# Running a block pipeline, and the next batch's attention, earlier in a one-core attention and mixture-of-experts kernel

## The chip, the cores and the metric

The kernel runs on one core of a Trainium2 chip. The time is the device time of one execution in microseconds (us). The median of the kernel before is 515.28 us; its profiled execution has a span of 514.3 us, and the time is one to two microseconds above the span. Ratios between kernels are the mean time of one kernel's fast runs over the mean of the other's fast runs in the same rounds, so they are not quite the ratio of the medians quoted beside them. The experiments ran in three groups, each on one chip and with runs of the kernel before beside them: tie, gate_early, pool_first and before_tail; left_last, pool_best, pool_best2 and pool_best2_gate; after_again, pool_best3 and no_late_w.

The engines are PE (matmul), PEld (its weight loads), DVE (vector), ACT (scalar), POOL and SP (here only a queue that issues DMA).

## The reference, cut to what matters

```python
# linear attention over 8 batches, 8 heads, 576 tokens, 64 columns
phi = lambda x: where(x > 0, x, exp(x) - 1) + 1
kv  = einsum('bhsd,bhse->bhde', phi(k), v);  z = sum(phi(k), axis=2)
x   = einsum('bhsd,bhde->bhse', phi(q), kv) / (phi(q) @ z + 1e-6)   # -> 4608 tokens x 512
# four experts, every token goes through all of them
for e in range(4):
    out += p[:, e:e+1] * (relu(x @ w1[e]) @ w2[e])      # w1 512x1024, w2 1024x512
```

## The kernel before

The 4608 tokens are nine tiles of 512. Tile j is 512 tokens of batch j; tile 8 holds the 64 "leftover" tokens of each batch. A unit (j, e) is one expert on one tile. It has a first layer, a hidden activation `h`, and a second layer that adds into `acc`.

There are two ways to compute a unit. The plain one takes 32 matmuls of 512 columns in each layer. The other takes seven block products instead of eight (a Strassen-like scheme): 56 matmuls of 256 columns in each layer, plus sums of blocks. The class `Block` is half a first layer in that scheme; `layer2_product` is a piece of the second.

```python
class Block:                       # cut
    def p1(self): ... self.products(self.b, ...); self.e5 = self.bank("e"); nc.scalar.copy(self.e5, self.b)
    def p2(self): ... nc.scalar.activation(self.h[:, :, 0, 0:NH], self.e5, AF.Relu)
    def p6(self): ... self.u2 = self.copy("u2", 2)          # ACT copies PSUM to SBUF
    def p7(self): ... self.u3 = self.copy("u3", 1)
    def p5(self): ...
    def c22(self): add_relu(self.h[:, :, 1, NH:NT], self.e5, self.u3)   # DVE
    def p4(self): ... nc.scalar.activation(..., AF.Relu)
    def p3(self): ... add_relu(self.h[:, :, 0, NH:NT], self.e5, self.u2)
```

The kernel before uses the plain scheme for all of tile 0 and for unit (1, 0), and the block scheme for the other 31 units. Batch 1's attention runs near the end of tile 0, and batch 2's is pressed into the last three units of tile 1. From tile 2 on there is a steady state. Work is put at positions counted in slots (one block product each), sorted, and emitted between block products.

```python
def run(end):
    while work and work[-1][0] < end:          # strictly below the next slot
        g = work.pop()[2]; g[0](*g[1:])
slot = 0
for n in range(len(blocks) + 1):
    ...
    for own, name in ((True,"p1"),(False,"p7"),(False,"p5"),(True,"p2"),(False,"p4"),(True,"p6"),(False,"p3")):
        getattr(x, name)(); ...
        slot += 1
        run(slot)
```

The weights are loaded, and cast from 32-bit to 16-bit, by DMA issued from POOL. Batch 1's inputs are issued from POOL too, behind all weights. Inputs of the later batches, and all outputs, go through the SP queue:

```python
for r in range(6): load_w(0, r)                 # weights, POOL queue
for e in range(1, E):
    for r in range(4): load_w(e, r)
b1.load_left("k", "v", "q", eng=nc.gpsimd)      # batch 1, POOL queue, behind them
for (n, i), home in zip(ORDER, homes): b1.load(n, i, nc.gpsimd, home=home)
```

In the second layer of the block scheme, a running sum and a side sum share one bank of PSUM (the memory, divided into banks, that the matmuls write to): `run, side = pys[i][:, 0:DH], pys[i][:, DH:Dm]`.

## Time and profile before

| stretch (us) | what runs | length | PE work, counted | PE gap |
|---|---|---|---|---|
| 24.08 to 64.23 | tile 0, plain | 40.15 | 40.17 | 0.0 |
| 64.23 to 93.73 | batch 1's attention, last of tile 0, first layer of (1, 0) | 29.50 | 24.33 | 5.2 |
| 93.73 to 136.83 | block pipeline fills, batch 2's attention | 43.10 | 34.30 | 8.8 |
| 136.83 to 149.37 | first unit of tile 2 | 12.54 | 12.23 | 0.3 |
| 149.37 to 486.88 | to the last block | 337.51 | 335.55 | 2.0 |

"PE work, counted" is a sum over the matmul records of the stretch: 0.216 us for each of 512 columns, 0.109 for 256, and about 0.056 for the small ones of the attention. These are the distances from start to start in full stretches of the PE's timeline. The gap is the length less that sum. I count this way because the page's busy time of the PE overstates: records overlap, and a matmul at half clock counts as busier.

The first fence is from the page of the kernel before: the span in 40 slices of 12.86 us, in tenths (PE busy, granted PE clock, DMA share), and the GB/s that the DMA engines moved.

```profile
PE   6799978889999999999999999999999999999994
PEclk9799999998999999999999999999999999999998
DMA  8999933737254425452445244623231020001003
GB/s 251 208 208 207 228 123 124 213 114 119 48 164 144 106 58 146 144 110 57 145 144 110 55 144 145 108 45 118 83 67 27 2 83 1 1 22 63 1 1 83
```

The second is the busy time by stretches of the same kernel. The columns are the stretch, its length, the busy time (and number of instructions) of PE, PEld, DVE, ACT and POOL, then granted clock, DMA share and GB/s. The DMA share adds up the times of all packets, so it can pass 1.

```profile
24.08:64.23 40.15, 40.15 (x190) 18.35 (x189) 18.16 (x32) 18.32 (x31) 14.36 (x21) 1.00 1.11 213
64.23:93.73 29.50, 25.36 (x165) 13.18 (x164) 19.58 (x50) 18.75 (x39) 7.43 (x12) 1.00 0.46 148
93.73:136.83 43.10, 38.07 (x305) 28.70 (x304) 31.31 (x63) 31.21 (x63) 20.41 (x17) 0.96 0.52 116
136.83:188.50 51.67, 51.46 (x488) 45.76 (x486) 41.69 (x92) 38.10 (x78) 41.79 (x39) 1.00 0.43 116
```

From 137 us on the PE is full. The room for a gain lies between 64 and 137 us. And until about 64 us the DMA engines are full at some 207 GB/s.

The third fence is the end of the PE's timeline. Columns: start, length, engine, line, operation, output<-inputs, size, count.

```profile
500.62 1.33 PE L611 MATMUL py<-t,hs 128*128 128x256 f16 x8
501.80 1.33 PE L611 MATMUL py<-w,h 128*128 128x256 f16 x8
502.96 1.33 PE L611 MATMUL py<-t,hs 128*128 128x256 f16 x8
```

A pair of products takes 1.17 us from start to start, where eight matmuls need 0.87.

### The profile page before, as it was taken

How to read it: one execution, taken by the hardware profiler on the slowest of the kernel's cores; microseconds unless marked ns; L12 is line 12 of the kernel's file. 1: busy time of each engine (PE TensorE's matmuls, PEld its weight loads, DVE VectorE, ACT ScalarE, POOL GpSimd, SP SyncE). 2: the span in 40 equal slices, each digit the busy share in tenths (PEclk: the TensorE clock that was granted, in tenths of full speed). 3: DMA queues.
4: the chain of work that ended last, by engine and by line, in shares of the span. 5: the costliest groups of instructions: out<-in, count | busy, mean ns of one | idle time of the engine just before them, and what ended most of it. 6: DMA issues, size and time to landing. Idle time of an engine off the chain costs nothing.

```text
span 514.3 us, 11256 instructions
## 1 busy us (share of the span) xinstructions
PE 489.0 (95%) x4199; PEld 397.7 (77%) x4199; DVE 366.0 (71%) x787; ACT 324.2 (63%) x647; POOL 345.8 (67%) x340
## 2 busy tenths in 40 slices
PE   6799978889999999999999999999999999999994
PEld 3444444467788888898889888888988888888873
DVE  5544586359986879687968796889688756775684
ACT  5653475995589559955895599559954465446520
POOL 2522522146796698669866986698668977987781
PEclk9799999998999999999999999999999999999998
DMA  8999933737254425452445244623231020001003
GB/s 251 208 208 207 228 123 124 213 114 119 48 164 144 106 58 146 144 110 57 145 144 110 55 144 145 108 45 118 83 67 27 2 83 1 1 22 63 1 1 83
DMA packets 80935, 54.29 MB, mean 106 GB/s; under 512 B 46224, under 2 KB 73872, under 8 KB 80880
## 3 DMA queue, kind: packets, MB, share of 16 engines
q1 hardware_dynamic: 71760, 41.64, 30.8%
q0 software_dynamic: 9120, 11.93, 12.0%
q8 instruction: 33, 0.54, 0.4%
q14 instruction: 22, 0.18, 0.1%
HBM read 45.16 MB, written 9.44 MB: 106 GB/s over the span
## 4 chain that ended last, share of the span: by engine, by line
PE 80%; DVE 8%; ACT 5%; DMA 2%; issue 2%; SPq 2%; DVEq 0%; ACTq 0%
PE py L611 34%; PE pb L673 19%; PE pe L673 14%; PE ph L472 5%; PE py L527 5%; DVE acc L518 3%; DVE x_sb L397 2%; PE psum_kv L374 1%; DMA rawu<-in_v_dram 1%; SPq L239 1%; DMA qT<-qp 1%; PE psum_nd L414 1%; DVE h L657 1%; ACT u L684 1%; ACT vp L295 1%
## 5 line engine op out<-in xcount | busy, mean ns | idle before, releaser
L518 DVE SCALAR_TENSOR_TENSOR acc<-py,p_sb,acc 128x256 f32<-128x256 f32 (+1 forms) x390 | 184.0, 487 | 62.0 <-PE py L611 48.9
L583 POOL TENSOR_TENSOR hs<-h 128x512 f16<-128x512 f16 x62 | 72.0, 1161 | 67.7 <-DVE h L657 67.7
L657 DVE CUSTOM_DVE_ANT_0 h<-pe,u 128x512 f16<-128x512 f32 x124 | 85.4, 689 | 36.2 <-PE pe L673 19.1
L673 PEld LDWEIGHTS <-w 128*128 128x128 f16 x992 | 96.3, 98 | 16.3 <-issue 2.9
L611 PEld LDWEIGHTS <-h 128*128 128x128 f16 x992 | 97.3, 98 | 14.9 <-issue 2.7
L611 PE MATMUL py<-w,h 128*128 128x256 f16 x744 | 107.4, 274 | 0.7 <-DVE acc L518 0.2
L585 POOL TENSOR_TENSOR hs<-hs,h 128x512 f16<-128x512 f16 x62 | 71.7, 1156 | 24.8 <-PE py L611 22.2
L684 ACT COPY u<-pb 128x512 f32<-128x512 f32 x124 | 73.1, 590 | 22.4 <-PE pb L673 20.0
L611 PEld LDWEIGHTS <-hs 128*128 128x128 f16 x744 | 71.8, 98 | 11.3 <-issue 2.9
L673 PEld LDWEIGHTS <-s 128*128 128x128 f16 x744 | 72.5, 98 | 9.3
L611 PE MATMUL py<-t,hs 128*128 128x256 f16 x496 | 74.4, 272 | 1.2 <-DVE acc L518 1.0
L673 PE MATMUL pb<-tt,w 128*128 128x256 f16 x496 | 74.6, 273 | 0.9 <-ACT u L684 0.9
L589 POOL TENSOR_TENSOR hs<-h,hs 128x512 f16<-128x512 f16 x62 | 71.7, 1157 | 3.2 <-PE py L611 3.2
L587 POOL TENSOR_TENSOR h<-h 128x512 f16<-128x512 f16 x62 | 72.2, 1164 | 0.0
L699 ACT ACTIVATE h<-pe 128x512 f16<-128x512 f32 x62 | 37.0, 598 | 53.2 <-PE pe L673 52.6
L693 ACT COPY pe<-pb 128x512 f32<-128x512 f32 x62 | 35.9, 579 | 46.7 <-PE pb L673 43.1
L527 PE MATMUL py<-w,h 128*128 128x512 f16 x160 | 38.4, 379 | 0.8 <-DVE acc L518 0.8
L472 PE MATMUL ph<-xT,w 128*128 128x512 f16 x160 | 38.3, 387 | 0.9 <-ACT xT L451 0.9
L717 ACT ACTIVATE h<-pb 128x512 f16<-128x512 f32 x62 | 36.9, 595 | 1.3 <-PE pb L673 1.2
L673 PE MATMUL pe<-tt,s 128*128 128x256 f16 x248 | 37.5, 274 | 0.0
L673 PE MATMUL pb<-tt,s 128*128 128x256 f16 x248 | 37.2, 273 | 0.0
L516 ACT ACTIVATE acc<-py,p_sb 128x256 f32<-128x256 f32 (+1 forms) x64 | 31.4, 508 | 7.5 <-PE py L527 4.2
(102 smaller groups left out, 635.0 us busy)
## 6 DMA issues: line engine op xcount, KB each, us to landing
out_dram<-acc SPq DMA_DIRECT2D x32, 256.0 KB, 2.4
w<-in_moe_w_dram POOLq DMA_DIRECT2D x14, 512.0 KB, 19.6
rawb<-in_v_dram SPq DMA_DIRECT2D x26, 256.0 KB, 2.9
rawb<-in_q_dram SPq DMA_DIRECT2D x26, 256.0 KB, 2.9
rawb<-in_k_dram SPq DMA_DIRECT2D x26, 256.0 KB, 2.8
w<-in_moe_w_dram POOLq DMA_DIRECT2D x4, 256.0 KB, 7.2
rawb<-in_v_dram POOLq DMA_DIRECT2D x4, 256.0 KB, 3.6
out_dram<-acc SPq DMA_DIRECT2D x8, 128.0 KB, 2.3
```

What stands on the lines that cost most here:

```text
L472: nc.tensor.matmul(out=ph, lhsT=w1_sb[e][:, dc, fj * P : (fj + 1) * P], rhs=xT_of(j)[:, dc], start=(dc == 0), stop=(dc == DC - 1),)
L518: nc.vector.scalar_tensor_tensor(out=acc, in0=ps, scalar=pscal, in1=acc, op0=AO.mult, op1=AO.add)
L527: nc.tensor.matmul(out=py, lhsT=rows(hT, fj)[:, ns * P : (ns + 1) * P], rhs=w2_sb[e][:, fj, :], start=(fj == 0), stop=(fj == FC - 1),)
L583: nc.gpsimd.tensor_tensor(out=hs[0], in0=a21, in1=a22, op=AO.add)
L585: nc.gpsimd.tensor_tensor(out=hs[1], in0=hs[0], in1=a11, op=AO.subtract)
L587: nc.gpsimd.tensor_tensor(out=a21, in0=a11, in1=a21, op=AO.subtract)
L589: nc.gpsimd.tensor_tensor(out=hs[3], in0=a12, in1=hs[1], op=AO.subtract)
L611: nc.tensor.matmul(out=ps, lhsT=lhsT(k), rhs=rhs[:, k], start=first and k == 0, stop=k == FH - 1, skip_group_check=True,)
L657: nc.vector._custom_dve(TENSOR_ADD_SAT, out=out, in0=ps, in1=u, s0=BIG, s1=0.0)
L673: nc.tensor.matmul(out=ps[:, kk], lhsT=lk(kc), rhs=rhs[:, kc], start=first and kk == 0 and kc == 0, stop=kc == 1, skip_group_check=True,)
L684: nc.scalar.copy(u, self.b)
L699: nc.scalar.activation(self.h[:, :, 0, 0:NH], self.e5, AF.Relu)
```

## The change

The intent is to start the block pipeline at tile 0's second expert. Tile 0's plain second layers then feed the PE while the pipeline fills. Batch 1's attention is spread over the slots of tile 0, batch 2's gets the steady schedule, and the last unit gets separate PSUM banks. Batch 1's loads move to the SP queue, behind a small DMA that reads a finished `h` (a gate). The diff, cut to its core (the tuned numbers of the positions are mostly left out):

```diff
+    "DMA": ('w100', 'w101', 'w102', 'w103', 'w220', 'w200', 'w201', 'w110', 'w111', 'w121', 'w120',
+            'w210', 'w211', 'w130', 'w131', 'w221', 'w230', 'w231'),      # layer, expert, piece
+    "WGATE": ('q', 3),
+    "BLK": (-1.0, 7.0, 14.0, 21.0, 28.0, 35.0, 53.0),
 ...                                       # ATTN[0], batch 1: k from 21.9, lk 19.9, v from 26.0, q from 33.4
+            g=(14.1, 14.3),
+    def load_first():                      # weights start when q's last piece of batch 0 is there
+        nc.gpsimd.tensor_copy(out=scr[:, 0:1], in_=b0.raw[tuple(CFG["WGATE"])][:, 0, 0, 0:1])
+        for x in CFG["DMA"]: load_w(*map(int, x[1:]))
+    def gate(i):
+        nc.sync.dma_start(out=scr[0:1, ...], in_=latest["h"][0:1, 0, 0, 0:8].bitcast(FP32))
-        b1.load_left("k", "v", "q", eng=nc.gpsimd)
-            b1.load(n, i, nc.gpsimd, home=home)
+            put(at["g"][0], bt.load_left, "k", "v", "q")              # SP queue, behind the gate
+                put(at["g"][n == "q"], bt.load, n, i, nc.sync, homes[m])
-            if self.b >= 2:                # phi of batch 1: Identity and Exp on ACT, one DVE pass
+            if self.b >= 1:
 ...                                       # qT and xT of batch 1: PE transposes, evacuated by ACT
+        if (j, e) == (NTILES - 1, E - 1):  # last unit: running and side sums in separate banks
+            if p == 2:
+                pys[i] = [ppm.tile([P, DH], FP32, tag=tag, bufs=2, name=f"p{tag}") for tag in ("b", "e")]
+            run, side = pys[i]
+        def put_block(at, *g):             # block products are now entries of the same sorted list
+            for pos, name in ((0,"p1"),(3,"p2"),(5,"p6"),(8,"p7"),(9,"p5"),(9.1,"c22"),(11,"p4"),(13,"p3")):
+                put_at(at + pos, getattr(bl, name))
 ...
         work.sort(key=lambda w: w[0:2])
+        for _, _, g in work: g[0](*g[1:])
```

## The prediction

> **What bounds the kernel now.** From 137 us on, the PE: busy time by stretches shows PE at 51.46 of 51.67 us for one tile at full clock (DVE 41.7, ACT 38.1, POOL 41.8). The Trainium skill ("Perfetto Trace Analysis", Identifying the Most-Contended Engine) calls matmul busy time a bad measure, so I count issue times from the PE's timeline: 0.216 us per N=512 matmul, 0.109 per N=256, about 0.055 per small attention matmul.
> - 24.08 to 64.23 us (tile 0, plain): full.
> - 64.23 to 93.73 (batch 1's attention, last tile-0 expert, tile 1's first layer 1): 24.4 us of work in 29.5, 5 us of bubbles. The waits name late batch-1 data (PE waits 2.6 us for the POOL cast of vl) and ACT/DVE chains.
> - 93.73 to 136.83 (block pipeline fills; plain layer 2, weight sums and batch 2's attention squeezed in): 34.2 us of work in 43.1, 9 us of bubbles.
> - Tail, 499.4 to 507.7: product pairs take 1.17 us where the PE needs 0.87. Running and side sums share one PSUM bank, so PE and DVE alternate, as the skill ("PSUM — Partial Sum Buffer", PSUM bank collisions) says two engines on one bank must.
>
> **What the change does.**
> 1. Layer 1 of tile 0's experts 1 to 3 and both layers of tile 1's expert 0 go from 32 N=512 matmuls (6.91 us) to 56 N=256 (6.1): about -3.8 us of PE work net of extra transposes, all on the critical path.
> 2. The pipeline fills while tile 0's plain layer 2 feeds the PE, batch 1's attention spreads over 36 slots, batch 2 gets the steady schedule. Most of the 14 us of bubbles should go.
> 3. Costs: batch 1's phi takes an extra 0.64 us ACT pass (8 times), qT/xT evacuations go to ACT (0.59 each), tile 0's token sums to DVE; six blocks take 2.95 us ACT and 1.38 us DVE each; nearly all 32 weight sums (0.68 to 0.92 us) must fit before tile 1. In the batch-1 stretch I estimate ACT 31 and DVE 33 us against 31 us of PE work, with all attention going through two PSUM banks. Remaining bubbles: 6 us (estimate).
> 4. DMA: weights start when q's last piece is in (about 10 us, as before); 8.4 MB at the 207 GB/s of the page's slices end near 52 us, about 5 us ahead of use. Batch 1's 3.1 MB waits on the SP queue for a gate at about 42 us and shares with the last weights.
> 5. Start: six small loads leave the SP queue (0.63 us each); v's last piece (15.3 us, on the chain) comes about 0.7 us sooner.
> 6. Tail: separate banks make pairs DVE-bound, 2 x 0.46; 7 pairs save 1.65 us.
>
> Sum, as span: 23.4 (dense layer 1 starts) + 108.0 (PE work up to the second unit of tile 2; 111.8 before) + 6 (bubbles) + 363.3 (rest, less tail) = 500.7; plus 0.9 between span and time: 501.5 us, 2.7% faster. Range 497 to 507. Chances: faster by over 2% 0.82, within 2% 0.17, slower by over 2% 0.01.
>
> **What would show it.** Tile 1 as a 51.7 us stretch with PE full; second unit of tile 2 starting near 137 us instead of 149.4; bubbles of about 6 us between 45 and 80 us, released by ACT and DVE; tail pairs at 0.93 us; first dense layer 1 at about 23.4.
>
> **What would make it wrong.** The batch-1 stretch saturating ACT/DVE or its two banks (12 us of bubbles or more gives 507); weights late for the blocks, whose sums need the whole matrix (the out-of-order w2 half costs 2.5 us); the gate opening late; granted clock falling after PE gaps (0.80 to 0.85 in some early stretches before).

## The result, and the profile after

The changed kernel takes 522.94 us (median of 4 runs, 522.69 to 525.18) against 515.28. The ratio is 1.0157, with a 95% interval of 1.0129 to 1.0186. It is slower by 1.6%; I had forecast a gain of 2.7% and a range of 497 to 507 us. The profiled span is 521.0 us, against 500.7 in my sum.

The same rows of the page, after (slices of 13.03 us):

```profile
PE   5887499989999999999999999999999999999994
PEclk9999599999999999999999999999999999999998
DMA  8999943535244425452444354624222020002003
```

The fifth slice, 52 to 65 us, has the PE at 0.4 and its clock at 0.5, and the DMA still at 0.9. By stretches, with the boundaries at the same events as before (start of dense matmuls, first block of unit (1, 0) at 92.83, second unit of tile 2 at 154.18):

```profile
22.65:50.20 27.55, 24.07 (x151) 14.14 (x151) 13.24 (x26) 15.29 (x30) 4.69 (x7) 1.00 1.18 208
50.20:66.93 16.73, 7.29 (x22) 3.10 (x22) 4.95 (x9) 6.90 (x14) 0.00 (x0) 0.59 1.08 244
66.93:92.83 25.90, 24.51 (x203) 16.55 (x202) 22.98 (x48) 19.49 (x42) 0.00 (x0) 1.00 0.37 107
92.83:115.77 22.94, 20.77 (x170) 15.29 (x167) 16.12 (x27) 22.09 (x49) 14.96 (x13) 1.00 0.51 162
```

In the second row no engine is loaded: ACT 6.90 and DVE 4.95 of 16.73 us. So the stretch is not bound by any of them. By count the PE did 3.90 us of work there and lost 12.8. ACT's waits between 45 and 70 us (total, number and longest) are

```profile
ACT kp L301 <- DMA rawb<-in_k_dram: 7.5, 1, 7.5
ACT kl L340 <- DMA rl<-in_k_dram: 4.5, 2, 3.4
```

and the PE's longest between 20 and 110 us

```profile
PE pb L722 <- ACT u L733: 6.3, 3, 5.6
PE pe L722 <- ACT pe L742: 3.9, 1, 3.9
```

ACT stands 12 us at batch 1's k, which has not come. The PE does not need that k yet. It needs ACT's copies `u` and `pe` of a block of unit (0, 2), and those stand behind k in ACT's queue. The PE's timeline shows both waits:

```profile
54.06 1.01 PE L722 MATMUL pe<-xT,w 128*128 128x256 f16 x4 [3.87 <-ACT pe L742]
54.87 2.77 PE L571 MATMUL py<-w,h 128*128 128x512 f16 x6
63.22 1.01 PE L722 MATMUL pb<-tt,w 128*128 128x256 f16 x4 [5.58 <-ACT u L733]
```

These two waits are 9.4 of the 12.8 us. The other 3.4 us are matmuls between and after them that took about twice their time, start to start (0.43 us instead of 0.216).

The DMA view between 43 and 58 us shows why k is late. q0 carries the weights and q1 batch 1's loads; the columns are packets, MB, and share of the 16 engines' time:

```profile
q0 software_dynamic: 2105, 2.60, 98.0%
q1 hardware_dynamic: 1622, 0.40, 20.5%
rawb<-in_k_dram SPq DMA_DIRECT2D x4, 256.0 KB, 11.4
```

In 15 us the SP queue got 0.40 MB through, 27 GB/s of some 200. That is about what the six leftover loads hold (six times 64 KB), which stand first in the queue; the first 256 KB piece of k, issued at 47.35 us, reached ACT at 61.5. The pieces of k took 11.4 us from issue to landing (median of four), where the whole run's median is 3.0.

There are two more losses. Between 28 and 50 us 4.8 us are lost by count (17.05 us of work in 21.82); the PE's longer waits there are for weights (2.1 us in all) and for a sum of weights on DVE (1.2 us). And one that I had not thought of: the steady tiles, which the change was not to touch, take 52.01 us instead of 51.42. The PE's timeline at the second unit of tile 2, before:

```profile
149.81 0.60 PE L611 MATMUL py<-w,h 128*128 128x256 f16 x4
150.32 0.60 PE L673 MATMUL pb<-tt,w 128*128 128x256 f16 x4
150.76 0.60 PE L611 MATMUL py<-t,hs 128*128 128x256 f16 x4
```

and after:

```profile
154.61 0.60 PE L660 MATMUL py<-w,h 128*128 128x256 f16 x4
155.43 0.60 PE L660 MATMUL py<-t,hs 128*128 128x256 f16 x4 [0.22 <-DVE acc L562]
155.86 0.60 PE L722 MATMUL pb<-tt,w 128*128 128x256 f16 x4
```

Two products have changed places, and the one now in front waits for DVE. Positions 9.0 and 10.0 of the second layer fall exactly on slots of block products. A layer-2 product of unit n at 9.0 stands at base + 14n + 20 + 9, and `p7` of the next unit's second block at base + 14(n+1) + 7 + 8, which is the same number. The old loop let the block product go first, because it ran only work strictly below the next slot. The new sorted list breaks a tie by order of insertion, and unit n's products are inserted before unit n+1's blocks.

The tail does what was expected of it:

```profile
509.08 1.04 PE L660 MATMUL pe<-t,hs 128*128 128x256 f16 x8
509.95 1.04 PE L660 MATMUL pb<-t,hs 128*128 128x256 f16 x8
510.83 1.21 PE L660 MATMUL pe<-w,hs 128*128 128x256 f16 x8
```

Pairs follow each other after 0.87 us instead of 1.17; only the last two intervals are longer, 1.04 and 1.18 us.

### The profile page after: what moved, and what is told of

Its sections match the earlier page's. It is cut to its first block, busy times and chain, and to the rows that moved or that the text cites. A ratio compares the mean times of both kernels' runs of the same rounds, so it can differ in the third digit from the quotient of the medians.

```text
span 521.0 us, 11542 instructions
## 1 busy us (share of the span) xinstructions
PE 487.7 (94%) x4327; PEld 408.4 (78%) x4327; DVE 375.6 (72%) x800; ACT 336.0 (65%) x679; POOL 345.8 (66%) x328
## 4 chain that ended last, share of the span: by engine, by line
PE 78%; DMA 9%; ACT 5%; DVE 2%; issue 2%; SPq 2%; POOL 1%; ACTq 0%; DVEq 0%
PE py L660 35%; PE pb L722 21%; PE pe L722 16%; DMA w<-in_moe_w_dram 3%; DMA rawb<-in_k_dram 3%; PE py L571 2%; DMA rawb<-in_q_dram 2%; DVE acc L562 1%; PE psum_nd L458 1%; DMA qT<-qp 1%; PE psum_kv L418 1%; SPq L244 1%; ACT vp L322 1%; ACT u L733 1%; SPq L264 1%
## 5 line engine op out<-in xcount | busy, mean ns | idle before, releaser
L722 PEld LDWEIGHTS <-w 128*128 128x128 f16 x1120 | 108.4, 98 | 30.8 <-issue 14.2
L706 DVE CUSTOM_DVE_ANT_0 h<-pe,u 128x512 f16<-128x512 f32 x140 | 96.6, 690 | 48.9 <-PE pe L722 28.4
L733 ACT COPY u<-pb 128x512 f32<-128x512 f32 x140 | 82.5, 589 | 34.4 <-PE pb L722 32.4
L722 PEld LDWEIGHTS <-s 128*128 128x128 f16 x840 | 81.9, 98 | 13.5 <-DVE s L599 1.7
L722 PE MATMUL pb<-tt,w 128*128 128x256 f16 x560 | 84.4, 273 | 7.4 <-ACT u L733 7.4
L748 ACT ACTIVATE h<-pe 128x512 f16<-128x512 f32 x70 | 41.8, 597 | 48.0 <-PE pe L722 47.5
L722 PE MATMUL pb<-tt,s 128*128 128x256 f16 x280 | 42.0, 273 | 1.2 <-DVE s L599 1.2
L767 ACT ACTIVATE h<-pb 128x512 f16<-128x512 f32 x70 | 41.7, 596 | 1.3 <-PE pb L722 1.2
L722 PE MATMUL pe<-xT,w 128*128 128x256 f16 x248 | 37.6, 275 | 4.5 <-ACT pe L742 3.9
L722 PE MATMUL pb<-xT,w 128*128 128x256 f16 x248 | 37.2, 272 | 0.7 <-DMA w<-in_moe_w_dram 0.5
```

The lines of the kernel that those rows point to most:

```text
L706: nc.vector._custom_dve(TENSOR_ADD_SAT, out=out, in0=ps, in1=u, s0=BIG, s1=0.0)
L722: nc.tensor.matmul(out=ps[:, kk], lhsT=lk(kc), rhs=rhs[:, kc], start=first and kk == 0 and kc == 0, stop=kc == 1, skip_group_check=True,)
L733: nc.scalar.copy(u, self.b)
L767: nc.scalar.activation(self.h[:, :, 1, 0:NH], self.b, AF.Relu)
```

## The experiments

Theory A: the loads of batch 1 share the DMA engines with the weights, so their data are late, and the in-order ACT passes the delay on to the blocks. Rival B, from my own list of what could make me wrong: ACT, DVE and the two PSUM banks of the attention saturate in that stretch, whatever the data do. Rival C: the gate simply opens too late.

The table gathers the PE gaps by count, in us. "dense start" is where full matmuls begin (22.7 to 24.2 us); U is the first block of unit (1, 0); V is the second unit of tile 2, which ends the part that the change rearranged.

| kernel | time | ratio to before | dense start to 50 us | 50 to 70 | 70 to U | U and 3 blocks more | dense start to V | V to last block |
|---|---|---|---|---|---|---|---|---|
| before | 515.28 | 1 | | | | | 14.3 | 2.0 |
| changed | 522.94 | 1.0157 | 4.6 | 13.0 | 2.7 | 2.9 | 23.7 | 4.8 |
| after_again | 523.57 | 1.0175 | 3.8 | 14.4 | 2.8 | 3.0 | 24.4 | 4.6 |
| tie | 520.66 | 1.0110 | 3.5 | 13.9 | 2.8 | 2.9 | 23.7 | 1.9 |
| gate_early | 520.46 | 1.0111 | 3.0 | 10.1 | 2.7 | 3.0 | 19.4 | 5.0 |
| left_last | 523.67 | 1.0179 | 4.9 | 11.4 | 4.4 | 3.0 | 24.3 | 5.2 |
| pool_first | 514.78 | 1.0000 | 4.0 | 5.3 | 2.2 | 3.1 | 15.2 | 4.5 |
| pool_best | 511.48 | 0.9948 | 3.7 | 5.1 | 2.2 | 3.0 | 14.2 | 1.9 |
| pool_best2 | 510.81 | 0.9932 | 1.9 | 7.5 | 2.0 | 2.9 | 14.7 | 1.7 |
| pool_best2_gate | 510.47 | 0.9929 | 2.0 | 6.3 | 2.0 | 3.1 | 13.7 | 1.6 |
| pool_best3 | 510.39 | 0.9918 | 1.8 | 6.8 | 2.1 | 3.0 | 14.1 | 2.1 |
| no_late_w (wrong result) | 507.16 | 0.9858 | 2.0 | 3.3 | 2.0 | 2.9 | 10.8 | 1.7 |

### after_again: the changed kernel on another occasion

No edit. It ran on the same chip as pool_best3 and no_late_w.

> The changed kernel unaltered, on the chip of the two runs beside it. Expected: 522 to 524 us, with the same large PE gap of 12 to 14 us between 50 and 70 us; if the gap is absent here, the cause is the chip and not the program.

It took 523.57 us (ratio 1.0175, 1.0152 to 1.0198), with 14.4 us of gap between 50 and 70 us. The gap belongs to the program.

### tie: the exact tie undone

```diff
-    "L2AT": (3.7, 3.8, 5.4, 6.6, 7.1, 8.3, 9.0, 10.0, 12.1, ...),
+    "L2AT": (3.7, 3.8, 5.4, 6.6, 7.1, 8.3, 9.01, 10.01, 12.1, ...),
```

> The changed kernel with two layer-2 positions moved from 9.0 and 10.0 to 9.01 and 10.01, so that the block's seventh product is again issued before the sixth layer-2 product, as in the kernel before. Theory (the new queue of work breaks an exact tie the other way, and the PE then waits about 0.3 us per unit for DVE): the tile period falls from 52.0 to 51.4 us, the drift of 2.6 us between tile 2 and the last block goes, time 520 us (2.5 to 4 us under the changed kernel). Rival (the drift comes from something else, such as DMA or the removed memset): no change, 523 us.

It took 520.66 us. The ratio to before is 1.0110 (1.0086 to 1.0134), against 1.0157 for the changed kernel. A steady tile, by stretches, first of the kernel before, then of the changed kernel, then of this one:

```profile
194.95:246.37 51.42, 51.42 (x490) 46.08 (x488) 40.97 (x90) 38.02 (x79) 40.83 (x39) 1.00 0.43 114
```

```profile
200.07:252.08 52.01, 51.79 (x490) 46.06 (x488) 41.11 (x90) 38.26 (x79) 40.64 (x38) 1.00 0.42 113
```

```profile
202.10:253.50 51.40, 51.40 (x489) 45.89 (x487) 40.84 (x90) 37.88 (x79) 39.86 (x37) 1.00 0.43 114
```

From V to the last block it needs 337.34 us instead of 340.14 (2.8 less), which is about the 337.51 of the kernel before. The drift came from the tie, and nothing else is needed to explain it. The intervals of the two ratios just touch, so it is the trace that shows this, and the time agrees.

### gate_early: the gate 12 slots earlier

```diff
-            g=(14.1, 14.3),
+            g=(2.5, 2.7),
```

> The changed kernel with both gates of batch 1's loads at slot 2.5 instead of 14.1: the loads go to the SP queue at about 36 us instead of 42.5. Theory A (the loads share the DMA engines with the weight queue and get only about a sixth of them until the weights end near 58 us): the first k piece still lands after 55 us, the PE's large gap shrinks by 1 to 4 us only, 519 to 523 us. Rival C (the gate simply opens too late): k lands 6 us earlier, the gap shrinks by 6 us or more, 517 us or less.

It took 520.46 us. The first loads were issued at 37.9 us instead of 42.7, about 5 us earlier, and the gap between dense start and V shrank by 4.3 us, of which 2.9 between 50 and 70 us. ACT still stands at k between 45 and 70 us:

```profile
ACT kp L301 <- DMA rawb<-in_k_dram: 9.6, 3, 8.7
```

The first piece of k was issued at 41.9 us and reached ACT at 58.2, only 3.3 us earlier than in the changed kernel. So an earlier gate helps a little, about as theory A said; the data still crawl. Rival C, taken alone, falls.

### pool_first: batch 1's loads in the POOL queue, among the weights

```diff
-    "DMA": (..., 'w130', 'w131', 'w221', 'w230', 'w231'),
+    "DMA": (..., 'w130', 'w131'),
+    "DMA2": ('left', 'b0-7', 'w221', 'b7-12', 'w230', 'w231'),   # b0-7: batch 1's first seven pieces
+    def load_more(): ...            # issues DMA2 in this order, all from nc.gpsimd
-                put(at["g"][i], gate, i)
-            put(at["g"][0], bt.load_left, "k", "v", "q")
-                put(at["g"][n == "q"], bt.load, n, i, nc.sync, homes[m])
+        put_at(-20.0, load_more)
```

> The changed kernel with batch 1's loads taken off the SP queue and put into the POOL queue: its first seven pieces right after the first-layer weights of expert 3 and before the last three weight pieces, the others before the last two. Theory A (sharing with the weight queue makes the data late and the in-order ACT waits): no ACT wait of over 2 us for batch 1's k, the PE gap of 12.8 us between 50 and 67 us falls under 4 us, 512 to 515 us. Rival B (ACT, DVE and two PSUM banks saturate in that stretch whatever the data does): the gap stays above 8 us, released by ACT and DVE lines, 519 us or more.

It took 514.78 us, 8.2 us less than the changed kernel and equal to the kernel before (ratio 1.0000, 0.9978 to 1.0023). The order of instructions on ACT, DVE and PE is, instruction for instruction in the two traces, that of the changed kernel; only which queue carries batch 1's loads, and behind what, is different. ACT's waits for data between 45 and 70 us are now

```profile
ACT kl L354 <- DMA rl<-in_k_dram: 3.3, 1, 3.3
ACT kp L315 <- DMA rawb<-in_k_dram: 0.4, 1, 0.4
```

and the gap between 50 and 70 us is 5.3 us instead of 13.0 (I had said under 4, and no wait of over 2 us for k; the leftover k took 3.3). Most of the loss is theory A's. Rival B expected over 8 us.

### left_last: the same queue, large packets first

```diff
-            put(at["g"][0], bt.load_left, "k", "v", "q")          # 256-byte runs
             for m, (n, i) in enumerate(mine):
                 put(at["g"][n == "q"], bt.load, n, i, nc.sync, homes[m])
+                if m == 5: put(at["g"][0], bt.load_left, "k", "v", "q")
-            lk=19.9, lkd=20.6,
+            lk=26.85, lkd=26.87,
```

> The changed kernel, still on the SP queue behind the same gate, but with the six leftover loads (256-byte runs) issued after the first six 1 KB-run loads of k and v instead of before them (and the leftover k phi moved behind the k phis). Theory A2 (two busy queues share the DMA engines packet by packet, so what the SP queue gets in bytes depends on its packet size; the leftovers' small packets use up 8 us): the first k piece lands within 6 us of its issue instead of about 12, all four by about 54 us; the ACT wait of 7.5 us for k shrinks under 3 us, total 518 to 521 us against 522.9. Rival (the SP queue gets a fixed small share of the bytes): k lands only 1 to 3 us earlier, total unchanged.

Here the direction held, and neither the sizes nor the total did. The first piece of k was there 8.6 us after its issue (6 expected; 14.2 in the changed kernel) and the fourth at 58.4 us (54 expected); ACT's waits for k fell from 7.5 to 3.9 us (under 3 expected). The DMA view of this kernel between 43 and 58 us:

```profile
q0 software_dynamic: 1776, 2.28, 85.4%
q1 hardware_dynamic: 1264, 1.22, 29.9%
```

In packets the SP queue's part is what it was: 1264 of 3040, or 42%, against 1622 of 3727, or 44%. In bytes it is three times as much, 1.22 MB instead of 0.40. So the rival (a fixed part of the bytes) falls, although its forecast of the time, unchanged, came true. The Trainium skill ("DMA: Bandwidth & Descriptors", Queues, rings and completion order) says that each DMA engine goes round between the queues it has work for, a packet at a time. Both windows fit that: nearly equal counts, very unequal bytes. But the same section takes a packet to be some 9 to 17 descriptors, and what the profile counts as packets of this queue are on average 247 and 965 bytes, about one run each; that the two are the same is not shown. ACT passed its last k wait at 58.4 us, where the changed kernel only got its first k at 61.5. But nothing was gained in time, 523.67 us. ACT's longest wait between 45 and 70 us is now

```profile
ACT qlp L340 <- DMA rl<-in_q_dram: 5.7, 1, 5.7
```

and the PE's longest up to 110 us

```profile
PE psum_kv L418 <- DVE kl L356: 8.6, 1, 8.6
```

The leftovers, now last, were late instead, and the k-times-v product needs them. Having k early gained nothing here, as long as the leftovers came late.

### pool_best, pool_best2, pool_best2_gate, pool_best3: loads in the order of first use

All have the tie undone. With respect to pool_first:

```diff
 # pool_best: the out-of-order 'w220' goes behind batch 1's first seven pieces
+    "DMA2": ('left', 'b0-7', 'w220', 'w221', 'b7-12', 'w230', 'w231'),
 # pool_best2: k and the leftovers ahead of expert 3's first-layer weights
+    "DMA2": ('left', 'b0-4', 'w130', 'w131', 'b4-7', 'w220', 'w221', 'b7-12', 'w230', 'w231'),
 # pool_best2_gate: pool_best2 with
+    "WGATE": ('v', 1),
 # pool_best3: pool_best2_gate with v's last piece (7) ahead of 'w220'
+    "DMA2": ('left', 'b0-4', 'w130', 'w131', 'b4-8', 'w220', 'w221', 'b8-12', 'w230', 'w231'),
```

> Batch 1's loads in the POOL queue as in the run before, the out-of-order half of expert 2's second-layer weights moved behind them, and the tie undone. Theory: against 514.8 us the tie gives 2.7, the earlier weights 2 (the DMA waits of the first blocks and of layer 2 go), a little from the earlier k: 509 us. Rival B (ACT, DVE and PSUM banks bound this stretch): only the tie's 2.7, 512 us.

> As pool_best, with the first four k pieces and the leftovers ahead of expert 3's first-layer weights, so that each load is issued in the order of its first use. Theory: the ACT waits for batch 1's data fall under 1 us in total, PE gaps from the dense start to the second unit of tile 2 fall to about 9 us, 506 to 508 us. Rival B: no faster than pool_best.

> As pool_best2, with the weights' start tied to v's second piece instead of q's last (about 3 us earlier). If the weights' start limits the first blocks: 1 to 2 us faster. If the weights then delay batch 0's last pieces by as much: no change, or slower.

> As pool_best2_gate, with v's last piece (which the second half of k-times-v needs) ahead of expert 2's second-layer weights instead of behind them. Theory (what still stalls the stretch is the order in which data arrive): the 3.2 us wait for v goes, total 507 to 508.5 us. Rival B (engines and PSUM banks bound the stretch): no change, 510 us.

pool_best took 511.48 us (509 expected): by count the tie gave 2.6 us and everything else 1.0. pool_best2 took 510.81 (506 to 508 expected), with 4.4 us of ACT waits for v where I had said under 1 in total. The gap before 50 us fell from 3.7 to 1.9 us, and the one after rose from 5.1 to 7.5: the wait for weights turned into a wait for v. pool_best2_gate took 510.47, no clear difference. In pool_best3, 510.39 us (507 to 508.5 expected), the PE's direct wait for v went, but ACT (its waits between 45 and 70 us) still stands at v and then at q:

```profile
ACT vp L336 <- DMA rawb<-in_v_dram: 3.0, 1, 3.0
ACT qp L315 <- DMA rawb<-in_q_dram: 1.6, 1, 1.6
```

Its busy time by stretches between 50 and 70 us:

```profile
50.00:70.00 20.00, 15.40 (x109) 10.45 (x108) 13.59 (x23) 14.34 (x33) 5.75 (x8) 0.91 1.13 254
```

The DMA share is still 1.13 there. Each reordering helps one load and delays another. In time, pool_best (512), pool_best2 (no faster) and pool_best3 (510) came out at rival B's figures and not at mine. So what the reordering gained beyond pool_first and the tie is not clear of the noise, and these runs alone don't say whether data or engines limit the stretch; the next run takes that up. pool_best3 has the lowest median of the correct kernels: it beats the kernel before by 0.8% (ratio 0.9918, 0.9895 to 0.9941). The intervals of the four overlap, so the order among them is open.

### no_late_w: a quarter of the weights not loaded (wrong)

```diff
+            if e >= 2: nc.gpsimd.memset(w2_sb[e][:, fs], 0.02)
+            else:      nc.gpsimd.dma_start(out=w2_sb[e][:, fs], in_=w2_src[e, :, fs])
```

> As pool_best3, but the second-layer weights of experts 2 and 3 (2 MB of 8.4) are filled with a constant on POOL instead of loaded; the result is wrong on purpose. It shows what the DMA still costs in the best order. Theory A: the weight-related waits after 50 us go, PE gaps between 50 and 70 us fall to 3 us or less, what stays is ACT and DVE's part, 503 to 506 us. Rival B: within 1 us of pool_best3.

It took 507.16 us (503 to 506 expected), 3.2 less than pool_best3. The gap between 50 and 70 us fell from 6.8 to 3.3. Rival B's figure, within 1 us of pool_best3, fails here. So about 3 us of what pool_best3 loses is still the DMA engines' capacity. The other columns moved by 0.4 us at most. One ACT wait of 1.8 us for v is left. Most of what stays, 10.8 us in all from dense start to V, comes with no wait for data that the PE's view of waits names. Between 90 and 100 us, where 2.2 us are lost by count, ACT is the most loaded of the engines that feed the PE:

```profile
90.00:100.00 10.00, 8.23 (x77) 6.53 (x76) 6.53 (x11) 9.36 (x23) 5.97 (x5) 1.00 0.51 164
```

There ACT is busy 9.36 of 10 us. How the 10.8 us divide among ACT, DVE and the PSUM banks was not tried.

### before_tail: the new tail alone, in the kernel before

```diff
+        if (j, e) == (NTILES - 1, E - 1):
+            if p == 2:
+                pys[i] = [ppm.tile([P, DH], FP32, tag=tag, bufs=2, name=f"p{tag}") for tag in ("b", "e")]
+            run, side = pys[i]
 ...                                       # product 1 starts the running sum of this unit afresh
+            order = L2ORD if n < len(units) - 1 else (2, 1, 5, 6, 3, 7, 4)
```

> The kernel before with only the new tail (running and side sums of the last unit in separate banks, and its product order). Theory: pairs fall from 1.17 to 0.87-0.93 us, gain 1.2 us, 514.0 us. Rival (the last pieces are bound by the hidden sums on POOL or by the stores): no gain, 515.2 us.

It took 513.93 us. The ratio is 0.9984 (0.9961 to 1.0007), so the time alone is not clear of the noise. In the trace, the stretch from the start of the last block to the start of the last matmul is 19.05 us instead of 20.66, which is 1.6 less. That is shown in the trace and only suggested by the time. The new tail changes both the banks and the order of the products; no run separates the two.

## Why the prediction was wrong

My sum was 500.7 us of span; the span is 521.0. Term by term:

| term of the sum | predicted | measured | difference |
|---|---|---|---|
| dense matmuls start | 23.4 | 22.65 | -0.75 |
| PE work up to the second unit of tile 2 | 108.0 | 107.83 | -0.2 |
| bubbles in that part | 6 | 23.70 | +17.7 |
| the rest, with the new tail | 363.3 | 366.8 | +3.5 |

The differences add to 20.3.

- **Point 1, the PE work removed, was nearly right.** The count fell from 111.03 to 107.83 us, by 3.2 for 3.8 predicted.
- **Point 5 is not borne out.** The dense start at 22.65 us looks like a gain, but v's last piece, which was to come 0.7 us sooner, landed at 16.05 us instead of 15.31 (15.1 to 15.3 in the two profiles with the old start, 15.9 to 16.3 in all with the new one). And the dense start scatters as much as that: 22.65 to 24.2 us with the new start, 22.78 (before_tail) and 24.08 with the old. The 0.75 us in the table is luck.
- **Point 6 was right about the bank, wrong about what comes next.** I had the pairs DVE-bound at 0.93 us; most fell to 0.87, which is what the PE itself needs. The Trainium skill ("PSUM — Partial Sum Buffer", PSUM bank collisions) says two engines must not be in one bank at once; the alternation in the trace, 1.17 us in one bank and 0.87 in two, agrees. The saving from the last block's start to the last matmul is 1.17 us in the changed kernel (19.49 against 20.66) and 1.6 in before_tail, for 1.65 predicted.
- **Point 4 is the step that failed**: "Batch 1's 3.1 MB waits on the SP queue for a gate at about 42 us and shares with the last weights." The gate time was right (41.6 us). "Shares" hid the error. I had put a time on the weights, which saturate the engines, and none on the loads added to the same engines. I had also left out the six leftover loads (0.39 MB), which went first and took nearly all of what the queue got. The loads got 27 GB/s in the 15 us that mattered, ACT stood at k or its leftovers for 12 of the 13.7 us up to 61.5, and being in order it held the blocks' copies back: 9.4 us of PE waits, and 3.4 us of half clock after them. The Trainium skill ("Trainium Kernel Development and Optimization", Key Constraints) says that DMAs of all issuing queues run on the same 16 engines. I had that at hand and used it only for the weights. Putting the loads into the weights' own queue, in order, gained 8.2 us, more than the change's whole loss of 7.7.
- **A second miss of point 4**: "8.4 MB ... end near 52 us, about 5 us ahead of use." The weights started at 12.94 us, not 10, and their last piece landed at 61.4 (57.9 before, where they started at 10.65 and no loads of batch 1 ran beside them). The first blocks and second layers had gaps of 4.8 us between 28 and 50 us; the waits there name weights, and a weight sum on DVE. Issuing in order of use cut the gap before 50 us from 3.7 to 1.9 us (pool_best to pool_best2).
- **Point 3, 6 us for the engines, may be nearly right; that is not shown.** The gaps that the DMA edits hardly moved are 2 us before U and 3 us after it, with some 3 more between 50 and 70 us in no_late_w; that ACT, DVE and the banks make them is my reading, no run tried it. And point 2's claim that "most of the 14 us of bubbles should go" failed: in the four reordered kernels they are 13.7 to 14.7 us. The bubbles of the kernel before were replaced by others in an earlier, DMA-limited stretch.
- **"363.3 (rest, less tail)" assumed that untouched code stays untouched.** The rewritten emission loop broke two exact ties the other way, which cost 2.8 us over the steady tiles (shown by tie; 2.6 against the kernel before). The tail's saving came 0.5 us short, and the time after the last matmul was 0.4 us longer; together that is the +3.5.
- **The falling clock** was named as a danger and came. In the 16.7 us of the gap the granted clock is 0.59; the six 512-column matmuls at 54.9 us take 2.77 us, about 0.43 each instead of 0.216. The Trainium skill ("TensorE: Matmul & The Clock Gate", Part 1) says an idle PE falls back to half its clock, which agrees: the PE had stood idle for 3.87 us before them. It is 3.4 of the 12.8 us and follows from the stall.

## What to carry to other kernels

Before moving work earlier, write down when its data can land, with everything that uses the DMA engines at that time in one list; a second issuing queue found no idle DMA engine here (201 GB/s with both queues busy from 43 to 58 us, some 207 with the weights alone), and it takes the choice of order out of your hands. An engine that works in order, as ACT does here, turns one late load into a stall of everything behind it, even of work that has its data, so a load's place in the instruction order is worth as much as its place in the queue. When an emission loop is rewritten, compare the order of instructions in the parts that were not to change: equal positions are decided by the sort.

## What the Trainium skill lacked or had wrong

- "DMA: Bandwidth & Descriptors" (Queues, rings and completion order) has the round by packets, but not what it does to a queue of small runs beside one of large ones: 44% of the packets, as the profile counts them, and 13% of the bytes (0.40 of 3.02 MB) with 256-byte runs first, 42% and 35% (1.22 of 3.52 MB) with 1 KB runs first.
- The same page's Bandwidth section gives no figure for loads that cast. Here weights cast from 32 to 16 bit run at about 207 GB/s as the profile counts them, by the bytes written: the eighteen weight pieces are 14 of 512 KB and 4 of 256 KB, half of what is read (so some 414 GB/s read, an estimate from this). With the weights nearly done, uncast loads reached some 310 to 390 GB/s between 60 and 64 us of the changed kernel.
- "Perfetto Trace Analysis" warns of matmul busy time and offers the FLOP share and weight-load time instead; no page that I read adds up start-to-start times into the work of a stretch, as is done here. In the worst stretch the PE's busy time was 7.29 us, the counted work 3.90.
- On an in-order engine that blocks others behind a late load, no page that I read has an example; here 12 us of ACT waiting for data became 9.4 us of PE waits and, with the half clock after them, 12.8 us of PE gap.
